# Splitting chained steps into single ones and writing out a new order of steps, in an SSD and feed-forward kernel

## The chip, the cores and the metric

The kernel runs on one core of one Trainium2 chip. A core has a matrix engine (TensorE, PE in the profile; its weight loads are listed as PEld), a vector engine (VectorE, DVE), a scalar engine (ScalarE, ACT), GpSimd (POOL) and a sync engine (SP), which in this kernel issues every transfer. Each engine works through its own instructions in the order in which the program gives them, and waits for the others by semaphores. The metric is the time of one execution on the device, in microseconds (us).

## The reference

First a state-space layer (Mamba-2, "SSD") over batch 4, 8 heads, 768 positions, head size 32, state size 16; then a gated feed-forward layer over the 3072 tokens that this gives, with 256 features and 1536 hidden ones:

```python
for c in range(nc):                                    # chunks of 32 positions
    cum = np.cumsum(la, axis=-1)                       # la = log of a
    L = np.exp(cum[:, :, :, None] - cum[:, :, None, :]) * causal
    M = np.einsum('bhin,bhjn->bhij', Cc, Bc) * L
    y_intra = np.einsum('bhij,bhjd->bhid', M, xc)
    y_inter = np.einsum('bhin,bhnd->bhid', Cc, state) * np.exp(cum)[:, :, :, None]
    y[:, :, sl] = y_intra + y_inter
    state = decay_full[:, :, None, None] * state + np.sum(Bx, axis=2)
...
rms = np.sqrt(np.mean(x * x, axis=-1, keepdims=True) + 1e-06)
xn = x / rms * rms_g
g = xn @ w_gate
silu = g * (1.0 / (1.0 + np.exp(-g)))
return silu * (xn @ w_val) @ w_out
```

The weights of the feed-forward layer arrive as 64-bit floating-point words; everything is computed in 32 bits.

## The kernel before, in words

**Blocks.** The 3072 tokens are six blocks of 512. Each block needs its part of the SSD (decays `L`, products `g` of B and C, states `A` and `S`, outputs `y`), then the norm (squares `sq`, their mean `ms` on PE, the root by ACT in `rs`, its spreading by transfers in `rb`, the normed tile `xn`), then the two input matrices (`gate` and `val`), the gating, and the output matrix.

**Weights.** The 64-bit words of 18 pieces are fetched and converted on the chip. Each piece k goes through `power(k)` (three dependent ACT steps, L217), `mantissa(k)` (two dependent DVE steps, L234 and L237) and `weight(k)` (one DVE step, L243, in steps called `wt`).

**Fast matrix products.** Most of the input products are done by a Strassen-like scheme: for each group j of 256 hidden features there are seven products `P.k.j` (L965) instead of eight. `P.1`, `P.4`, `P.6` and `P.7` add into one PSUM tile, `gate`, and `P.2`, `P.3` and `P.5` into another, `val`; there are two buffers of each. Between the products that add into `gate`, ACT copies the tile out (`take`, L971) and DVE adds such a copy to `val` (`C`, L977); then come the silu on ACT (L215) and the gating product (`hid`, L990, on DVE or POOL). A product is two 32-bit matmuls of 128x256, four in the profile. The sums of weights and of inputs that the scheme needs are L934 and L942. The output matrix has a scheme of its own: products `O` (L1086), sums of the hidden tiles (`u`, L1060) and totals (`w`, L1117 on DVE, L1113 on ACT), then `put`, the store. Part of block 0 is projected directly: `early` and `gate` steps (L879, L889), `norm` (L900), `hid` (L912) and `o` (L997).

**What sets the order.** No planner runs at build time. One string, `order`, lists the steps of the whole kernel, such as `0:P.1.5` (block slot 0, product 1 of group 5), and the loop at the end calls one function for each. Every engine, SP's transfers included, gets its instructions in that order. A number after a slash names the pair of PSUM banks for a step in the first part; after `switch` those banks hold the `gate` and `val` tiles. A step that issues several instructions puts them next to one another in their engine's queue. `rs.1` in slot 0, for example, is the square root of block 1's norm: Ln and Exp on ACT, and a transfer.

**The start.** `row sums` come first: `a` is loaded, turned (`aT`), limited (L351) and its logarithm taken; PE sums it (`r`), and `parts.0` (four dependent DVE steps, L411 to L417) splits the sums into three 16-bit parts; from these and a mask PE forms the exponents `e`, ACT the decays. In `order` the six loads of B and C (L143) stand near the beginning, then one pair of x, then `fetch.0` and `fetch.1`, which issue two transfers each (L185).

**ACT's tables.** `functions` (L202 to L209) remembers which set of functions is loaded, silu or exp and log, and puts in a load when a step needs the other one.

Of the kernel before, what the change touches and what calls it, by code (L numbers as in the profile page):

```python
# [10 lines left out]
I32 = mybir.dt.int32  # L11
# [9 lines left out]
def kernel(  # L21
# [195 lines left out]
    def power(k):  # L217
        words16, (lo, hi), dst, shape = fetched[k]
        n = shape[1] * shape[2]
        e = cvt.tile([P, n], FP32, tag="e", name="e", bufs=4)  # L220
# [3 lines left out]
        activation(out=k16, in_=words16, func=AF.Relu, scale=1.0 / 16, bias=kinks[:, 0:1])  # L224
        activation(out=g, in_=k16, func=AF.Prelu, scale=-1.0, bias=kinks[:, 1:2],
                             alpha=2.0 ** -20)
        activation(out=b16, in_=g, func=AF.Prelu, scale=-2.0 ** 27, bias=kinks[:, 2:3],
                             alpha=2.0 ** -20)
        parts[k, "e"] = b16.bitcast(BF16)

    def mantissa(k):
        words16, (lo, hi), dst, shape = fetched[k]
        m = cvt.tile(shape, I32, tag="m", name="m")
        nc.vector.tensor_scalar(out=m, in0=hi, scalar1=0xFFFFF, scalar2=0x100000,  # L234
                                op0=ALU.bitwise_and, op1=ALU.bitwise_or)
        parts[k, "f"] = f = m.bitcast(FP32)
        nc.vector.scalar_tensor_tensor(out=f, in0=lo.bitcast(U32), scalar=2.0 ** -32, in1=m,  # L237
                                       op0=ALU.mult, op1=ALU.add)
# [54 lines left out]
    def whole_chunks():  # L293
        nc.vector.memset(chunk_ones, 0.0)
        for u, r in enumerate(halves):
            nc.vector.memset(chunk_ones[r, u], 1.0)
# [12 lines left out]
    def of_quarters():  # L309
        nc.vector.tensor_scalar(out=three, in0=part[:, 3:4], scalar1=-1.0, scalar2=1.0,  # L310
                                op0=ALU.mult, op1=ALU.add)
        nc.vector.tensor_scalar_add(later_part, part[:, 0:1], -1.0)
        nc.vector.tensor_scalar(out=third_part, in0=part[:, 2:3], scalar1=-1.0, scalar2=None,
                                op0=ALU.mult)
# [4 lines left out]
    def from_middle():  # L319
        nc.vector.tensor_copy(out=mid, in_=upto)  # L320
        nc.vector.tensor_scalar_add(mid[0:HC], mid[0:HC], -1.0)

    def from_middles():
        nc.gpsimd.tensor_copy(out=mid, in_=upto)
        for r in halves:
# [3 lines left out]
        minus_mid()  # L329

    def mask16():
        for r in halves:
            nc.vector.tensor_copy(out=never16[r], in_=never[r, r])

    def kinks_of_powers():
        for k, v in enumerate((1152.0 - 7.5 / 16, 256.0, -1792.0 * 128.0)):
            nc.vector.memset(kinks[:, k:k + 1], v)
# [68 lines left out]
    def three_parts(k):  # L406
        r_ps = ps.pop(("r", k))
        room = nrm.tile([P, 4, P], FP32, tag="lead1", name="room", bufs=1)
        first, second = [room[:, k].bitcast(BF16).rearrange("p (s m) -> p s m", s=2)
                         for k in range(2)]  # L410
        nc.vector.tensor_copy(out=first, in_=r_ps)  # L411
        rest = room[:, 2:4]
        nc.vector.scalar_tensor_tensor(out=rest, in0=first, scalar=later_part, in1=r_ps,
                                       op0=ALU.mult, op1=ALU.add)
        nc.vector.tensor_copy(out=second, in_=rest)
        rows[k] = row = const.tile([P, 2, P], BF16, name="row%d" % k)
        nc.vector.scalar_tensor_tensor(out=row, in0=second, scalar=third_part, in1=rest,  # L417
                                       op0=ALU.mult, op1=ALU.add)
# [31 lines left out]
    def chunk_decays():  # L450
        activation(out=full.rearrange("p g h -> p (g h)"), in_=ps.pop("c"), func=AF.Exp)
        nc.gpsimd.tensor_tensor(out=fsel, in0=full,
# [52 lines left out]
    def causal(L):  # L505
        for r in halves:
            nc.gpsimd.affine_select(out=L[r], in_=L[r], pattern=[[0, L.shape[1]], [1, HC]],  # L507
                                    compare_op=ALU.is_ge, fill=0.0, base=0, channel_multiplier=-1)

    def spread(g):  # L510
        b, c = divmod(g, NC)
        o = (c * BH + b * NH) * HC
        for u, r in enumerate(halves):
            nc.sync.dma_start(out=pair_tile(g)[r].rearrange("p h m -> p (h m)"),
                              in_=rowv[u, o:o + NH * HC].partition_broadcast(HC))
# [8 lines left out]
    def exponential(g):  # L524
        L = pair_tile(g)
        activation(out=L, in_=L, func=AF.Exp)
        causal(L)

    def decays(g):
        subtract(g)  # L530
        exponential(g)
# [153 lines left out]
    def states(p):  # L685
        A_ps = ps.pop(("A", p))
        b, c0, chunks = chunks_of(p)
        new = ssd.tile([P, 2, 2, 2, D], FP32, tag="A", name="A")
        for u in range(2):
            n = sum(v == u for i, v in chunks)  # L690
            if n:
                nc.vector.tensor_tensor(
                    out=new[:, u, 0:n], in0=A_ps[u][:, 0:n],
# [799 lines left out]
```

## Time and profile before

| | |
|---|---|
| time, median of 3 runs (lowest, highest) | 391.32 us (391.13, 391.40) |
| span of the profiled execution | 389.5 us |
| PE busy | 383.3 us (98%) |
| DVE busy | 289.8 us (74%) |
| ACT busy | 226.4 us (58%) |
| POOL busy | 152.0 us (39%) |
| granted clock of PE | 1.00 throughout |

The span is one execution from its first to its last instruction as the profiler saw it; the time of a run is measured around the whole execution, 1.8 us more here. Times in rows count from the span's start. A row of the timeline gives start, length, engine, line, operation, output and inputs, and in brackets how long the engine had been idle and what it had been waiting for. Matmuls are pipelined: a group's length reaches beyond the start of the next one, and the distance from start to start is what the engine needs for one.

### The profile page before, as it was taken

To read this page: it belongs to the slowest core of one execution; us is meant where nothing else is said; L and a number is where in the kernel's file an instruction comes from. 1 tells how busy PE (TensorE), PEld (TensorE's weight loads), DVE (VectorE), ACT (ScalarE), POOL (GpSimd) and SP (SyncE) were. 2 spreads that over 40 slices of the span, in tenths; PEclk is the share of its full clock that TensorE was granted. 3 is DMA by queue.
4 is the path that set the end of the run, shared out by engine and by line. 5 is a ranking of instruction groups with operands and counts; after the bars stand their busy time and mean duration, and the time that the engine had idled before them with its cause. 6 is when DMAs were issued, how large, how long until landed. Compare 5 with 4: busy or idle time off the path is not lost.

```text
span 389.5 us, 9637 instructions
## 1 busy us (share of the span) xinstructions
PE 383.3 (98%) x3805; PEld 329.8 (85%) x3805; DVE 289.8 (74%) x612; ACT 226.4 (58%) x471; POOL 152.0 (39%) x168
## 2 busy tenths in 40 slices
PE   8999999999999999999999999999999999999996
PEld 5676478788888999888899988899888899988995
DVE  6999999997976988669594765768374577454684
ACT  2899979988767262665865234763444571345420
POOL 5022045523693455343577701364611234212231
PEclk9999999999999999999999999999999999999999
DMA  8978984474073414634336112000100001000001
GB/s 107 241 153 259 240 195 147 120 157 42 3 101 86 50 13 94 145 42 96 70 78 81 27 42 42 2 15 22 56 3 2 2 12 50 29 0 0 2 0 56
DMA packets 109940, 28.05 MB, mean 72 GB/s; under 512 B 94824, under 2 KB 103752, under 8 KB 109896
## 3 DMA queue, kind: packets, MB, share of 16 engines
q1 hardware_dynamic: 107816, 27.31, 32.8%
q8 instruction: 30, 0.49, 0.5%
q10 hardware_dynamic: 2080, 0.13, 0.4%
q14 instruction: 14, 0.11, 0.1%
HBM read 23.69 MB, written 3.74 MB: 70 GB/s over the span
## 4 chain that ended last, share of the span: by engine, by line
PE 87%; DVE 9%; issue 2%; ACT 1%; DVEq 0%; ACTq 0%
PE gate L965 29%; PE o L1086 23%; PE val L965 21%; PE o L997 5%; PE y L750 3%; PE g L613 1%; DVE wgv L243 1%; DVE m L237 1%; DVE m L234 1%; DVE hid L912 1%; PE g L606 1%; PE e L474 1%; PE y L678 1%; DVE L L652 1%; ACT yt L821 0%
## 5 line engine op out<-in xcount | busy, mean ns | idle before, releaser
L977 DVE TENSOR_TENSOR c<-val,p 128x512 f32<-128x512 f32 x99 | 67.4, 686 | 45.1 <-PE val L965 33.3
L971 ACT COPY p<-gate 128x512 f32<-128x512 f32 x99 | 56.8, 581 | 57.5 <-PE gate L965 55.4
L965 PE MATMUL gate<-tx,wgv 128*128 128x256 f32 x264 | 65.9, 381 | 0.0
L215 ACT ACTIVATE c<-c 128x256 f32<-128x256 f32 x99 | 40.0, 415 | 38.7 <-DVE c L977 38.4
L990 POOL TENSOR_TENSOR hid<-c 128x256 f32<-128x256 f32 x31 | 24.7, 800 | 87.1 <-ACT c L215 83.1
L965 PEld LDWEIGHTS gate<-tx,wgv 128*128 128x128 f32 x264 | 49.2, 190 | 7.3 <-ACT p L971 0.7
L1117 DVE TENSOR_TENSOR ob<-ob,o 128x128 f32<-128x128 f32 (+1 forms) x90 | 24.2, 298 | 21.7 <-PE o L1086 16.9
L990 DVE TENSOR_TENSOR hid<-c 128x256 f32<-128x256 f32 x68 | 34.5, 521 | 6.9 <-ACT c L215 6.7
L1086 PE MATMUL o<-two,hid 128*128 128x128 f32 x280 | 36.5, 276 | 0.1
L1086 PEld LDWEIGHTS o<-two,hid 128*128 128x128 f32 x280 | 34.5, 192 | 1.1 <-DVE hid L990 0.4
L965 PE MATMUL val<-xn,wgv 128*128 128x256 f32 x132 | 33.7, 381 | 0.0
L965 PE MATMUL val<-tx,sw 128*128 128x256 f32 x132 | 33.5, 380 | 0.0
L965 PE MATMUL val<-xn,sw 128*128 128x256 f32 x132 | 33.3, 381 | 0.0
L965 PE MATMUL gate<-tx,sw 128*128 128x256 f32 x132 | 33.1, 381 | 0.0
L965 PE MATMUL gate<-xn,wgv 128*128 128x256 f32 x132 | 32.8, 381 | 0.0
L507 POOL TENSOR_SCALAR_AFFINE_SELECT L<-L 64x512 f32<-64x512 f32 x32 | 23.6, 737 | 18.6 <-ACT L L215 17.4
L965 PEld LDWEIGHTS val<-xn,wgv 128*128 128x128 f32 x132 | 24.8, 190 | 3.5
L965 PEld LDWEIGHTS val<-tx,sw 128*128 128x128 f32 x132 | 24.8, 190 | 3.5 <-issue 0.2
L965 PEld LDWEIGHTS gate<-tx,sw 128*128 128x128 f32 x132 | 24.7, 190 | 3.5 <-ACT p L971 0.2
L965 PEld LDWEIGHTS gate<-xn,wgv 128*128 128x128 f32 x132 | 24.3, 190 | 3.4 <-DVE hid L912 0.3
L965 PEld LDWEIGHTS val<-xn,sw 128*128 128x128 f32 x132 | 24.4, 190 | 3.2 <-issue 0.2
L215 ACT ACTIVATE e<-e,kinks 128x512 f32<-128x512 int16 (+1 forms) x36 | 26.0, 722 | 1.2
(203 smaller groups left out, 717.0 us busy)
## 6 DMA issues: line engine op xcount, KB each, us to landing
L<-rowd SPq DMA_DIRECT2D x32, 128.0 KB, 3.4
xr<-in_x_dram SPq DMA_DIRECT2D x24, 128.0 KB, 3.2
wr<-in_moe_w_out_dram SPq DMA_DIRECT2D x6, 512.0 KB, 5.6
out_dram<-ob SPq DMA_DIRECT2D x24, 128.0 KB, 1.8
wr<-in_moe_w_gate_dram SPq DMA_DIRECT2D x5, 512.0 KB, 5.8
wr<-in_moe_w_val_dram SPq DMA_DIRECT2D x5, 512.0 KB
br<-in_B_dram SPq DMA_DIRECT2D x23, 64.0 KB, 2.6
dT<-rowe SPq DMA_DIRECT2D x10, 128.0 KB
```

The lines of the kernel that those rows point to most:

```text
L215: nc.scalar.activation(**operands)
L234: nc.vector.tensor_scalar(out=m, in0=hi, scalar1=0xFFFFF, scalar2=0x100000, op0=ALU.bitwise_and, op1=ALU.bitwise_or)
L237: nc.vector.scalar_tensor_tensor(out=f, in0=lo.bitcast(U32), scalar=2.0 ** -32, in1=m, op0=ALU.mult, op1=ALU.add)
L507: nc.gpsimd.affine_select(out=L[r], in_=L[r], pattern=[[0, L.shape[1]], [1, HC]], compare_op=ALU.is_ge, fill=0.0, base=0, channel_multipli ...
L750: nc.tensor.matmul(out=y[2 * k + u][rows, (2 * n + i) * HC:(2 * n + i + 1) * HC], start=(k, u, rows.start) not in opened, stop=True, skip_ ...
L965: nc.tensor.matmul(out=dst[:, half[w]], lhsT=lhsT, rhs=rhs, start=(k in (1, 2, 5) and w == 0), stop=True, skip_group_check=True)
L971: nc.scalar.copy(out=t, in_=Xs[j])
L977: nc.vector.tensor_tensor(out=t, in0=Zs[j], in1=a, op=ALU.add)
L990: engine.tensor_tensor(out=hid[:, 2 * j + c // 10 - 1, c % 10 - 1], in0=u, in1=src[:, half[1]], op=ALU.mult)
L997: nc.tensor.matmul(out=o, lhsT=hid[:, f, k // 2, (k % 2) * P:(k % 2 + 1) * P], rhs=wo[:, f], start=opens, stop=(f == NF - 1), skip_group_c ...
L1086: nc.tensor.matmul(out=Os[blk, b][:, place * P:(place + 1) * P], lhsT=hidden_or_sum(u)[:, g], rhs=rhs, start=(blk, b) not in opened, stop= ...
L1117: nc.vector.tensor_tensor(out=o, in0=o, in1=src, op=ALU.add if what[0] == "+" else ALU.subtract)
```

## The change

Functions that issue several instructions get an argument that picks one of them, and `order` names each separately. Split in this way are `power` (three), `mantissa` (two), `three_parts` (four), the constants of the start, the chunk decays (ACT step `cx`, POOL step `ch`), `exponential` (ACT step `ex`, and `ca`, the causal mask, for each half), `spread` (its two transfers), `states` (`Sn`, the new contributions, and `S`, one chunk each), `squares`, `taken_out` (`yt`), the norm's roots (`rs`), `norm_apply` (`xn`), `normed` and the last stores of block 0 (`putc`, `put`). The tile that a chain works on is now kept in a dictionary between its steps.

Then the whole string `order` is replaced. The instructions of PE, POOL and SP are the same ones in another order. DVE has one more (`xn` of block 0 in two halves), and ACT has 26 loads of a table instead of 22.

```diff
-    def mantissa(k):
+    def mantissa(k, stage):
         words16, (lo, hi), dst, shape = fetched[k]
-        m = cvt.tile(shape, I32, tag="m", name="m")
-        nc.vector.tensor_scalar(out=m, in0=hi, scalar1=0xFFFFF, scalar2=0x100000,
-                                op0=ALU.bitwise_and, op1=ALU.bitwise_or)
-        parts[k, "f"] = f = m.bitcast(FP32)
-        nc.vector.scalar_tensor_tensor(out=f, in0=lo.bitcast(U32), scalar=2.0 ** -32, in1=m,
-                                       op0=ALU.mult, op1=ALU.add)
+        if stage == 0:
+            parts[k, "m"] = m = cvt.tile(shape, I32, tag="m", name="m")
+            nc.vector.tensor_scalar(out=m, in0=hi, scalar1=0xFFFFF, scalar2=0x100000,
+                                    op0=ALU.bitwise_and, op1=ALU.bitwise_or)
+        else:
+            m = parts.pop((k, "m"))
+            parts[k, "f"] = f = m.bitcast(FP32)
+            nc.vector.scalar_tensor_tensor(out=f, in0=lo.bitcast(U32), scalar=2.0 ** -32, in1=m,
+                                           op0=ALU.mult, op1=ALU.add)
...
-    def states(p):
+    def states(p, n):
...
-    def norm_apply(blk):
+    def norm_apply(blk, t=0):
...
-            nc.vector.tensor_tensor(out=xns[0], in0=yts[0],
-                                    in1=r.unsqueeze(1).to_broadcast([P, 2, TB]), op=ALU.mult)
+            nc.vector.tensor_tensor(out=xns[0][:, t], in0=yts[0][:, t], in1=r, op=ALU.mult)
...
     order = """
-        0:warm 0:a 0:set 0:bc.0 0:ident 0:bc.1 0:bc2.1.1 0:ones 0:zeros 0:ident16 0:whole 0:kinks
-        0:idle.7 0:gcol 0:x.0 0:never 0:after 0:fetch.0 0:fetch.1 0:x.1 0:whole16 0:mask.0.0/0
-        0:part 0:hmask 0:upto 0:mid 0:mids 0:part2 0:aT 0:mask.1.1/2 0:la0 0:log4.0.4 0:upto2 0:r.0
-        0:fetch.2 0:head 0:sel 0:middles 0:after2 0:fetch.3 0:log4.4.2 0:log4.6.2 0:bc.3 0:tmask
-        0:parts.0 0:log 0:c*2 0:cx 0:mask.0.1/1 0:turn.0 0:Tb.0 0:T.0 0:d 0:dx 0:sums.0.1 0:sums.0.0
+        0:whole.0 0:warm 0:a 0:idle.7 0:ident 0:fetch.0 0:zeros 0:ones 0:ident16 0:kinks.1 0:upto
+        0:never 0:aT 0:whole16 0:fetch.1 0:mask.0.0/1 0:part 0:bc.0 0:whole.1 0:mid.0 0:upto2
+        0:mid.1 0:la0 0:kinks.0 0:never16.0 0:bc.1 0:never16.1 0:log4.0.4 0:mask.1.1/2 0:mids
+        0:whole.2 0:after 0:log 0:part2.2 0:bc2.1.1 0:r.0 0:part2.1 0:kinks.2 0:mask.0.1/0 0:part2.0
+        0:hmask 0:log4.6.2 0:after2 0:pow.0.0 0:head 0:man.0.0 0:log4.4.2 0:x.0 0:middles.0
+        0:parts.0.0 0:sel 0:parts.0.1 0:tmask 0:middles.1 0:d 0:parts.0.2 0:man.1.0 0:dx 0:middles.2
+        0:c*2 0:set 0:x.1 0:man.0.1 0:fetch.3 0:parts.0.3 0:pow.1.0 0:middles.3 0:r.1 0:cx 0:gcol
+        0:fetch.4 0:man.1.1 0:parts.1.0 0:fetch.5 0:scale.0.1 0:parts.1.1 0:sums.0.1 0:turn.0
...
-        0:silug.11.5 0:wt.12 0:hidgp.12.3 0:cw.0.1 0:ydone.2 0:silug.22.4 0:cw.1.2 0:fetch.17
-        0:spread.8 0:ms.1 0:take.6.5 0:P.7.5 0:rs.1 0:pow.13 0:sub.9 0:o.0/2 0:o.1 0:sub.10 0:man.13
-        0:fetch.14 0:hidg.21.4 0:take.7.5 0:wt.13 1:cwp.2.0 0:hidgp.22.3 0:cwp.0.3 0:C.22.5 0:P.4.5
+        0:sub.8 0:yt.3.2 0:man.14.0 0:ms.1 0:silug.21.4 0:take.6.5 0:rs.1.0 0:cwp.5.3 0:P.7.5
+        0:pow.15.1 0:rs.1.1 0:take.7.5 0:C.12.4 1:cwp.2.0 0:ex.10 0:o.0/2 0:P.4.5 0:pow.14.0
...
-        5:w.8 5:w.16 5:O.5.0 5:w.13 5:w.7 5:O.5.1 5:up.8 5:u.12 5:w.20 5:O.12.0 5:O.7.0 5:O.7.1
-        5:up.13 5:w.14 5:w.9 5:O.12.1 5:w.17 5:w.18 5:w.15 5:put.3 5:u.14 5:O.1.0 5:O.1.1 5:w.19
-        5:put.0 5:O.14.0 5:u.15 5:w.22 5:O.14.1 5:O.19.0 5:O.19.1 5:w.21 5:w.23 5:put.1 5:O.10.0
-        5:O.10.1 5:w.24 5:w.25 5:put.2
+        5:O.5.1 5:O.7.1 5:u.12 5:w.18 5:O.13.1 5:w.8 5:w.9 5:O.12.0 5:up.13 5:O.12.1 5:O.1.0 5:w.12
+        5:w.14 5:w.17 5:w.20 5:O.1.1 5:w.7 5:w.15 5:u.14 5:w.22 5:O.14.0 5:w.19 5:O.19.0 5:O.19.1
+        5:u.15 5:w.24 5:put.3 5:O.10.0 5:w.23 5:O.10.1 5:w.11 5:O.14.1 5:put.1 5:put.0 5:w.25 5:w.21
+        5:put.2
```

More of the change, by code (lines that the diff above doesn't have):

```diff
@@ L328, in from_middles, with mask16, kinks_of_powers @@
                                     scalar2=None, op0=ALU.add)
[L329 to L337, printed above, removed]
+    def mask16(k):
+        r = halves[k]
+        nc.vector.tensor_copy(out=never16[r], in_=never[r, r])
+    def kinks_of_powers(k):
+        nc.vector.memset(kinks[:, k:k + 1], (1152.0 - 7.5 / 16, 256.0, -1792.0 * 128.0)[k])
     def idle(n):
@@ L1144, in switch, with take @@
                          space=bass.MemoryType.PSUM))
[L1146 to L1151 removed]
+    def take(name):
+        return pair_of_banks(name, picks.pop(0))
     def start_decays(p, half=0):
[L1154 removed]
+        ps["e", p, half] = e = take("e")
         mask(p, e)
@@ L1223 @@
         "early": lambda f, s: products_early(
-            f, s, take("gate", ("gv", f)) if s == 0 else ps["gv", f]),
-        "norm": lambda f: (normed(f), leave(("gv", f))),
-        "gate": lambda f: products_gv(f, take("gate", ("gv", f))),
+            f, s, None if ("gv", f) in ps else take("gate")),
+        "norm": normed,
+        "gate": lambda f: products_gv(f, take("gate")),
         "silu": silu_of,
-        "hid": lambda f: (hidden(f), ("gv", f) in held and leave(("gv", f))),
+        "hid": hidden,
         "table": lambda k: functions("silu"), "switch": switch,
```

607 lines of the change are left out of this document (328 added, 279 removed).

## The prediction

> **What bounds the kernel now.** I read the span and the chain first, then busy time by stretch, then what DVE waits for, then DVE's, PE's and ACT's instructions one by one where the first big matrix products begin.
>
> From the page:
> ```profile
> span 389.5 us, 9637 instructions
> PE 87%; DVE 9%; issue 2%; ACT 1%; DVEq 0%; ACTq 0%
> ```
> The chain that ended last is PE for 87% of the span, and DVE's 9% is one stretch near the start. Busy time by stretch shows where (columns: stretch, length, then busy us and count for PE, PEld, DVE, ACT, POOL, then the clock, the DMA share, GB/s):
> ```profile
> 0.00:5.00 5.00, 3.86 (x13) 1.80 (x13) 3.14 (x21) 1.60 (x3) 2.41 (x12) 1.00 0.78 86
> 5.00:10.00 5.00, 4.91 (x38) 3.93 (x40) 3.47 (x11) 1.47 (x5) 2.60 (x5) 1.00 0.94 143
> 10.00:15.00 5.00, 5.00 (x64) 3.21 (x60) 4.57 (x11) 4.05 (x7) 0.00 (x0) 1.00 1.01 227
> 15.00:20.00 5.00, 4.35 (x112) 3.16 (x116) 4.78 (x11) 4.65 (x9) 0.00 (x0) 1.00 0.82 224
> 20.00:30.00 10.00, 9.93 (x150) 7.59 (x139) 9.59 (x23) 9.77 (x18) 2.18 (x2) 1.00 0.82 171
> 30.00:40.00 10.00, 9.96 (x61) 5.77 (x60) 9.86 (x18) 9.81 (x17) 2.25 (x3) 1.00 0.90 267
> 40.00:50.00 10.00, 10.00 (x141) 4.67 (x142) 9.69 (x22) 8.81 (x14) 0.00 (x0) 1.00 0.90 228
> 50.00:65.30 15.30, 14.80 (x286) 12.18 (x268) 14.69 (x32) 13.07 (x28) 9.04 (x11) 1.00 0.77 195
> ...
> 75.00:380.00 305.00, 304.85 (x2897) 274.40 (x2897) 216.22 (x436) 163.82 (x357) 129.38 (x131) 1.00 0.24 45
> ```
> DVE is full from 10 us until the products run, and idle before: 20 less 15.96 busy leaves 4.04 us of idle in the first 20, and 45.3 less 43.83 leaves 1.47 in the next 45.3. From 75 to 380 us PE is never without work (304.85 of 305.00). So only two things can move the time: when DVE gets its first 60 us of work done, and new stalls of PE later.
>
> What DVE waited for in 0 to 65.3 us (total, times, longest):
> ```profile
> DVE room L411 <- PE r_ps L402: 0.8, 1, 0.8
> DVE early L351 <- PE aT L347: 0.7, 1, 0.7
> DVE T L573 <- PE tp L554: 0.5, 1, 0.5
> ...
> DVE c L977 <- ACT p L971: 0.3, 1, 0.3
> DVE wgv L243 <- ACT e L215: 0.2, 1, 0.2
> ```
> The first three lie before 9 us. They and small gaps between dependent steps are the idle time.
>
> **Part one, the start.** The new order puts DVE steps that need nothing from the waited-for chain into those gaps: `mantissa` of pieces 0 and 1 (one L234 and one L237 each) and `parts.1` (four instructions, as `parts.0` has here). DVE's instructions, by start and length:
> ```profile
> 6.32 0.43 DVE L411 CAST room<-r_ps 128x256 bf16<-128x256 f32 x1 [0.83 <-PE r_ps L402]
> ...
> 7.70 0.48 DVE L417 SCALAR_TENSOR_TENSOR row<-room,third_part 128x256 bf16<-128x256 bf16 x1
> ...
> 60.86 0.69 DVE L237 SCALAR_TENSOR_TENSOR m<-wr,m 128x512 f32<-128x512 uint32 x1
> ...
> 62.07 0.69 DVE L243 SCALAR_TENSOR_TENSOR wgv<-m,e 128x512 f32<-128x512 f32 x1 [0.19 <-ACT e L215]
> 62.68 0.42 DVE L990 TENSOR_TENSOR hid<-c 128x256 f32<-128x256 f32 x1
> 63.02 0.69 DVE L977 TENSOR_TENSOR c<-val,p 128x512 f32<-128x512 f32 x1
> 63.62 0.68 DVE L912 TENSOR_TENSOR hid<-u,hid 128x512 f32<-128x512 f32 x1
> 64.22 0.41 DVE L990 TENSOR_TENSOR hid<-u,gate 128x256 f32<-128x256 f32 x1
> ...
> 65.55 1.24 DVE L702 SCALAR_TENSOR_TENSOR S<-S,fcol,A 128x64 f32<-128x64 f32 x4
> ...
> 68.47 0.42 DVE L234 TENSOR_SCALAR m<-wr 128x512 int32<-128x512 int32 x1
> 68.92 1.10 DVE L237 SCALAR_TENSOR_TENSOR m<-wr,m 128x512 f32<-128x512 uint32 x1
> ```
> Start to start, a 128x512 step takes 0.60 to 0.61 us of DVE (L243, L977, L912) and a 128x256 one 0.34, so `mantissa` twice is 2 x (0.42 + 0.61) = 2.1 us and `parts.1`, 6.32 to 8.18, at most 1.9: 4.0 us of filler against 4.04 of idle. It cannot all fit: the wait for the engine to start stays (0.89 us of `warm`), and the chain a, logarithm, row sums is as long as before. By hand 1.4 to 2.0 us of idle stay; I take **2.0 us won**, at most 2.6.
>
> The price is SP's queue. To have the weights by then, the four transfers of pieces 0 and 1 are issued ahead of six loads of B and C and the first of x:
> ```profile
> 7.51 0.58 SPq L185 DMA_DIRECT2D wr<-in_moe_w_gate_dram  x1
> ...
> 9.67 1.19 SPq L150 DMA_DIRECT2D xr<-in_x_dram  x2
> ```
> From 7.51 the four took 2.16 us to issue, so B and C start about that much later, behind 1 MB that the 227 GB/s of the 10 to 15 stretch moves in 4.6 us; DMA is already 0.78 to 1.01 busy. B and C of the first pair are needed after row 0 (8.18 us now, about 9.1 then, since `mantissa` stands ahead of `parts.0`), those of the second near 12.5. I find them about in time and charge nothing; if they are late by those 2.2 us, part one is worth nothing. That is the low end.
>
> **Part two, gaps between dependent steps.** Of the 1.47 us of idle from 20 to 65.3, the two named waits are 0.5; some 1.0 is gaps of 0.03 to 0.05 us (60.86 + 0.69 is already past the next start, 62.68 + 0.42 too, but a step that needs its predecessor's result starts only after it ends, as 68.92 after 68.47 + 0.42). With single steps another instruction stands between, and the last 0.08 us overlap. Between 0 and 1.0 I take **0.7 won**.
>
> **Part three, more work ahead of the tight point.** PE's instructions at the start of the products (start, length of the group, count):
> ```profile
> 65.29 1.03 PE L965 MATMUL gate<-xn,wgv 128*128 128x256 f32 x4
> 66.16 1.03 PE L965 MATMUL val<-xn,wgv 128*128 128x256 f32 x4
> ...
> 71.06 3.67 PE L997 MATMUL o<-wo,hid 128*128 128x256 f32 x16
> 74.75 1.13 PE L965 MATMUL gate<-tx,wgv 128*128 128x256 f32 x4
> ```
> The product at 65.29 (`P.1.5`) opens a gate tile that the `hid` sum at 64.22, done 64.63, must have left: 0.66 us of slack. In the new order DVE has, up to that same `hid`, two L234, one L237, one L243, one L520 and one L977 more, and one L702, one 128x256 L990 and one 128x256 weight sum less: 2 x 0.40 + 4 x 0.61 - 0.31 - 2 x 0.34 = 2.3 us more with the 0.06 that the split `xn` (two halves for one) adds. Beyond the slack that takes 2.3 - 0.66 = **1.6 us back**. So PE starts its unbroken run 2.0 + 0.7 - 1.6 = 1.1 us sooner. The L237 rows also show a price I leave at zero: the same step took 0.69 and 1.10, beside other work on POOL, and the new order may win or lose 0.4 at each such place.
>
> **Part four, ACT in the products.** A gate tile is copied by ACT (`take`, L971) before the next product may add to it. ACT's rows:
> ```profile
> 66.36 0.58 ACT L971 COPY p<-gate 128x512 f32<-128x512 f32 x1
> ...
> 70.06 1.28 ACT L209 ACT_TABLE_LOAD   x1
> 71.35 0.37 ACT L215 ACTIVATE r<-ms,eps 128x128 f32<-128x128 f32 x1
> 71.75 0.31 ACT L215 ACTIVATE r<-r 128x128 f32<-128x128 f32 x1
> 71.97 0.75 ACT L215 ACTIVATE e<-wr,kinks 128x512 int16<-128x512 int16 x1
> ...
> 74.13 0.56 ACT L971 COPY p<-gate 128x512 f32<-128x512 f32 x1
> ```
> The product of 65.29 is copied by 66.94; with one product between, PE, which starts a product every 0.87 us (65.29 to 66.16), would want the tile at 67.03. The old order has nearly always two products (1.73 us) or an `O` between; the new one has a single one at 19 places. With ACT free that costs nothing (0.09 less 0.06 to wake, as 74.69 to 74.75 shows); with an 0.37 ACT step in front it costs about 0.3. Bounds 0 to 19 x 0.3 = 5.7; I take 0.2, nearest to the free case, as ACT is busy 163.82 of 305 us, 54%, from 75 us on.
>
> Four table loads are added (22 to 26), 4 x 1.28 us on ACT. Three I find ahead of nothing that PE waits for, hidden by ACT's 46% of idle time; without that cover each would cost PE up to its 1.28. One, with Ln, a power step and Exp behind it, now stands directly ahead of the `take` that `P.4.5` waits for: 1.28 + 0.37 + 0.75 + 0.31 = 2.7 us. Before, PE already waited there (16 matmuls of 0.216 from 71.06 end at 74.52, the next came at 74.75). I take 0.2 more, bounds 0 to 0.6. The Trainium skill, page "ScalarE: Activation LUTs", section "What ACT_TABLE_LOAD costs", says that a switch costs 1283 ns and a drain of 1380 ns besides. The trace does not agree with the second: the load at 70.06 ended at 71.34 and Ln started at 71.35. By the page the stall would be 1.4 us larger.
>
> **Part five, the tail and the rest.** The end of block 5 is reordered as well:
> ```profile
> 382.51 1.16 PE L1086 MATMUL o<-sw,hid 128*128 128x128 f32 x8 [0.38 <-DVE ob L1117]
> ```
> As I read the order, the total L1117 that this product waits for now stands ahead of one more product, so the wait goes: 0.3 won, bounds 0 to 0.4. The last product, total and store are others than before but of the same kinds and lengths. Engines' work is otherwise the same instruction for instruction; finer steps of POOL and SP are hidden by PE after 65 us. If not, each late transfer would cost its issue, 0.5 us.
>
> **The sum.** -1.1 (start) + 0.2 (takes) + 0.2 (table) - 0.3 (tail) = -1.0 us. The profiled execution's span of 389.5 becomes 388.5. The median of the runs is 391.3, 1.8 more than the span, which I carry over: **390.4 us** (-0.2%). A measurement of this kernel can tell 0.2%, or 0.8 us, from no change: faster is under 390.5, slower over 392.1.
>
> **Rivals.**
> 1. The whole start pays: 2.6 + 1.0 - 1.6 = 2.0 less, and 0.3 at the tail, no stalls: 389.0. For it: the filler equals the idle time. Against: the chain of row sums has its own length.
> 2. No change: B and C land late by half of those 2.2 us, part one gives 1.0 instead of 2.0, and the sum is 0.0: 391.4. Late by all of it, the start costs 1.6 - 0.7 = 0.9, and the sum is +1.0, 392.3. For it: DMA share 0.94 to 1.01. Against: row 0, which comes first, is itself 0.9 later.
> 3. Slower, one mechanism: ACT arrives late at the 19 places with one product of cover. The sum without them is -1.2, so it turns the sign from 0.06 us a place and passes 0.2% from 0.1; at 0.2 it is 3.8 - 1.2 = +2.6, **393.9**, at the full 0.3 396. For it: a margin of 0.03 us. Against: ACT's mean load.
>
> By the page's drain the table load alone gives -1.0 + 1.4 = +0.4, 391.7, a case like rival 2; with the Ln row against it I give it 0.02 of that rival's chance.
>
> **How the numbers follow.** Forecast (389.4 to 390.9 by the bounds of its terms) 0.40, rival 1 0.16, rival 2 0.18, rival 3 0.26. The range, 388.2 to 393.6, reaches past rival 1's 389.0 by what the gaps of DVE could still give, and up to nearly the middle case of rival 3; above it lies about half of that rival, 0.14, below it 0.05. Faster: 0.16 and 0.33 of the 0.40, together 0.49; the same: the other 0.07 and 0.15 of rival 2, 0.22; slower: 0.26 and 0.03, 0.29.
>
> **What would show it.** In the new profile DVE should be busy some 18 of the first 20 us; the four weight transfers should precede B and C; the first unbroken products should stand about 1 us earlier; ACT should show 26 table loads. Waits of PE (or its weight loads) for ACT L971 totalling over 2 us, or DVE idle for transfers between 8 and 13 us, would make the forecast wrong.

## The result and the profile after

The changed kernel takes 421.07 us (median of 5 runs, 419.59 to 422.88) against 391.13 us (5 runs, 391.03 to 391.40): ratio 1.0775, 95% interval 1.0752 to 1.0798. The forecast was 390.4 us, with a range up to 393.6: the kernel is 30 us slower where a gain of 1 was expected. The profiled execution is the slowest of the five, 422.88 us with a span of 421.0; the other four have spans of 417.7 to 419.9.

From the page of the changed kernel (span, PE and its neighbours, granted clock in tenths over 40 slices, chain):

```profile
span 421.0 us, 9645 instructions
PE 393.8 (94%) x3805; PEld 330.9 (79%) x3805; DVE 297.7 (71%) x613; ACT 230.4 (55%) x475; POOL 154.6 (37%) x168
PEclk9998999998999999999999999989999999999999
PE 65%; DVE 12%; SPq 8%; DMA 7%; issue 3%; POOL 2%; ACT 2%; DVEq 0%; POOLq 0%; ACTq 0%
```

PE now stands in the chain for 65% instead of 87%, and two things are there that were not: SP's queue (SPq) with 8% and transfers (DMA) with 7%. PE is idle for 27.2 us instead of 6.2 (421.0 - 393.8, 389.5 - 383.3), and busy 10.5 us longer for the same 3805 matmuls. About 5 of the 10.5 are its clock, whose mean is 0.988 (421 x 0.012); what the rest is stays open. What PE waited for (total, times, longest):

```profile
PE val L1002 <- DVE xn L897: 5.2, 2, 3.9
PE o L1123 <- DVE ob L1154: 4.1, 4, 1.3
PE o L1123 <- DVE hid L1097: 2.9, 2, 2.5
PE y L700 <- DMA xr<-in_x_dram: 2.0, 2, 1.5
PE g L635 <- DVE T L609: 1.7, 1, 1.7
PE y L777 <- DVE L L674: 1.5, 1, 1.5
PE idle L359 <- DVE warm L385: 1.4, 1, 1.4
```

Before, four waits were listed, 2.5 us together. Now there are many, of many kinds, from one end of the kernel to the other. Busy time by stretch, the first and the long one as in the prediction (columns as there):

```profile
0.00:5.00 5.00, 3.55 (x13) 1.96 (x14) 2.79 (x22) 1.99 (x4) 2.34 (x12) 1.00 0.66 152
5.00:10.00 5.00, 4.43 (x34) 3.13 (x33) 4.15 (x13) 3.32 (x6) 2.47 (x5) 1.00 0.92 161
10.00:15.00 5.00, 4.27 (x54) 2.87 (x53) 4.91 (x11) 3.78 (x6) 0.92 (x1) 1.00 0.94 124
15.00:20.00 5.00, 5.00 (x83) 3.38 (x86) 4.42 (x11) 4.37 (x9) 0.00 (x0) 1.00 0.90 287
75.00:420.00 345.00, 327.84 (x2989) 287.47 (x2987) 235.72 (x468) 175.35 (x374) 133.48 (x133) 0.99 0.21 42
```

PE was never without work from 75 us on; now it is for 17.2 us (345 less 327.84).

**Where the time goes.** To place the loss I took PE's instructions of each kernel in their order, gave each the start-to-start time that its kind has in the trace of before, and called the sum the work. The lag is how much later than in the trace of before PE reaches the same amount of work, in us. Whether a kind is weighed by its mean or its median moves the entries by up to about 1 us, so smaller differences say nothing. The kernels beside the changed one are experiments of the next section.

| work done | changed | e3 | e4 | e5 |
|---|---|---|---|---|
| 30 | 0.2 | 0.0 | 0.1 | 0.2 |
| 60 | 8.7 | 4.0 | 4.5 | 3.4 |
| 80 | 14.9 | 11.6 | 4.5 | 5.3 |
| 100 | 14.9 | 11.6 | 12.5 | 5.6 |
| 140 | 17.1 | 11.6 | 14.7 | 7.9 |
| 180 | 22.1 | 13.0 | 19.4 | 14.1 |
| 220 | 24.0 | 13.0 | 21.4 | 16.1 |
| 260 | 30.6 | 13.0 | 26.6 | 22.7 |
| 360 | 31.3 | 12.9 | 27.3 | 23.4 |

The first 30 us of work take what they took, within that 1 us. The changed kernel's 8.7 at 60 has about 4 us of a wait at 39 us (the `T` L609 row above, and a low clock behind it) that the traces of e3, e5, e6, e7 and e10, which have the same order there, do not show: it comes and goes with one transfer, issued at 32.45 and landed at 38.64 here. Half of the loss is there by 80 us of work, the other half comes in single steps until 260. The largest step of the first half is at 86 to 98 us:

```profile
80.93 0.30 ACT L215 ACTIVATE r<-r 128x128 f32<-128x128 f32 x1
...
81.33 4.18 SPq L541 DMA_DIRECT2D L<-rowd  x6
85.61 0.54 SPq L883 DMA_DIRECT2D roots<-r  x1
...
86.88 0.69 DVE L547 TENSOR_TENSOR L<-L,tok 128x512 f32<-128x512 f32 x1 [3.34 <-DMA L<-rowd]
...
87.04 1.89 PE L1034 MATMUL o<-wo,hid 128*128 128x256 f32 x8
...
88.49 1.75 SPq L888 DMA_DIRECT2D sq<-roots  x4
...
91.99 1.41 DVE L897 SCALAR_TENSOR_TENSOR xn<-yt,gcol,sq 128x512 f32<-128x512 f32 x2 [1.83 <-DMA sq<-roots]
...
92.80 1.13 PE L1002 MATMUL val<-xn,wgv 128*128 128x256 f32 x4 [3.87 <-DVE xn L897]
94.06 3.67 PE L1034 MATMUL o<-wo,hid 128*128 128x256 f32 x8
```

The root of block 1's norm is done by ACT at 81.23. Its transfer to DRAM (`rs.1.2`, L883) is issued at 85.61, 4.4 us later, because SP is still issuing six spreads of decays (L541), 0.7 us each, that stand ahead of it. DVE, in its own order, stands at 86.88 behind a spread that landed late, then waits for the roots themselves; PE waits 3.87 us. The eight matmuls at 94.06 then take 3.67 us where the eight at 87.04 took 1.89: PE's clock has dropped to half. In the profile before, the same two transfers were:

```profile
72.09 0.35 SPq L847 DMA_DIRECT2D roots<-r  x1
...
74.20 1.95 SPq L852 DMA_DIRECT2D sq<-roots  x4
```

Counted in SP's rows (ACT's queue issues two more transfers, the first loads of B and C, so it is not quite all that SP issues), 64 transfers stood ahead of `roots` before, and 90 stand ahead of it now: 7 spreads, 12 squares, 4 of B, 2 of x and one weight more. Before, SP had nothing else to do and waited 8.8 us for the root; now the root waits 4.4 us for SP. The other 9.2 of the 13.5 us by which `roots` goes out later are the root's own lateness (done at 81.23 instead of 72.06), most of which the lag of 8.7 at 60 us of work already holds. In e3, which lacks the wait at 39 us, the root is done at 76.44 and issued at 81.63, 5.2 us later. The 13.5 us can't be divided into a price for each transfer: 72 of the 90 rows take 0.55 us on average, 18 are longer than 1 us, up to 4.26, and why these are longer is not shown. The DMA engines' share from 33 us to there (to 73 and to 86) rose from 0.70 to 0.83, with the same 183 and 184 GB/s.

### The profile page after: what moved, and what is told of

It is laid out like the page before. It is cut to its first block, busy times and chain, and to the rows that moved or that the text cites. A ratio compares the mean times of both kernels' runs of the same rounds, so it can differ in the third digit from the quotient of the medians.

```text
span 421.0 us, 9645 instructions
## 1 busy us (share of the span) xinstructions
PE 393.8 (94%) x3805; PEld 330.9 (79%) x3805; DVE 297.7 (71%) x613; ACT 230.4 (55%) x475; POOL 154.6 (37%) x168
## 4 chain that ended last, share of the span: by engine, by line
PE 65%; DVE 12%; SPq 8%; DMA 7%; issue 3%; POOL 2%; ACT 2%; DVEq 0%; POOLq 0%; ACTq 0%
PE gate L1002 22%; PE val L1002 15%; PE o L1123 14%; PE o L1034 4%; SPq L133 3%; PE gate L914 2%; DVE xn L897 2%; PE gate L926 2%; DMA dT<-rowe 1%; SPq L541 1%; DVE hid L1027 1%; PE g L635 1%; PE y L777 1%; DVE hid L1097 1%; DMA sq<-roots 1%
## 5 line engine op out<-in xcount | busy, mean ns | idle before, releaser
L1002 PE MATMUL gate<-tx,wgv 128*128 128x256 f32 x264 | 66.8, 384 | 0.0
L215 ACT ACTIVATE c<-c 128x256 f32<-128x256 f32 x99 | 38.8, 415 | 22.9 <-DVE c L1014 22.5
L1123 PE MATMUL o<-two,hid 128*128 128x128 f32 x280 | 39.4, 277 | 0.3 <-DVE hid L1097 0.3
L1123 PEld LDWEIGHTS o<-two,hid 128*128 128x128 f32 x280 | 35.7, 192 | 1.8 <-issue 0.6
L1002 PE MATMUL gate<-xn,wgv 128*128 128x256 f32 x132 | 34.3, 386 | 2.0 <-DVE hid L949 0.9
L1027 DVE TENSOR_TENSOR hid<-c 128x256 f32<-128x256 f32 x68 | 32.6, 492 | 4.7 <-ACT c L215 4.6
L1002 PE MATMUL val<-xn,sw 128*128 128x256 f32 x132 | 34.5, 388 | 1.0 <-DVE c L1014 1.0
```

Of the source, the lines that this page charges most:

```text
L215: nc.scalar.activation(**operands)
L1002: nc.tensor.matmul(out=dst[:, half[w]], lhsT=lhsT, rhs=rhs, start=(k in (1, 2, 5) and w == 0), stop=True, skip_group_check=True)
L1027: engine.tensor_tensor(out=hid[:, 2 * j + c // 10 - 1, c % 10 - 1], in0=u, in1=src[:, half[1]], op=ALU.mult)
L1123: nc.tensor.matmul(out=Os[blk, b][:, place * P:(place + 1) * P], lhsT=hidden_or_sum(u)[:, g], rhs=rhs, start=(blk, b) not in opened, stop= ...
```

## The experiments

**e1: splitting alone.** The order of before, with every split chain written as its single steps next to one another.

```diff
-        0:take.6.5 0:P.7.5 0:rs.1 0:pow.13 0:sub.9 ... 0:man.13
+        0:take.6.5 0:P.7.5 0:rs.1.0 0:rs.1.1 0:rs.1.2 0:pow.13.0 0:pow.13.1 0:pow.13.2 0:sub.9 ... 0:man.13.0 0:man.13.1
```

> The changed kernel's single steps, put in the order of the kernel before (each old step's single steps side by side; block 0's normed tile still in two halves). Theory A (the new order alone makes the loss, the splitting costs nothing): 391.1 within 0.5 us, 22 table loads. Theory B (the splitting itself costs, by the extra instruction and the way tiles are held between steps): a good part of the 30 us, over 400 us.

Measured: 391.28 us, ratio 1.0014 (0.9999 to 1.0028). DVE's extra instruction is there (x613), the stretches are those of before. That is theory A: at most 1 us of the 30 (the upper end of the interval) comes from the finer functions, the rest is the new order.

**e2 and e3: one half old, one half new.** The order was cut at the first products of the block after block 0 (about 92 us). e2 has the old order up to there and then what is left in the new order, e3 the reverse. In outline:

```diff
-    order = new
+    order = old up to 1:P.*.0, then the steps of new that are not yet done      (e2)
+    order = new up to 1:P.*.0, then the steps of old that are not yet done      (e3)
```

> The old order up to the first product of the next block (about 82 us), then all that is left in the new order. The new order falls behind by 14.9 us up to there, by PE's instructions against the same work in the kernel before. Theory A (the losses are local, each at its place): 421 - 15 = 406 us. Theory B (a queue that overflows at the start, SP's, drags on and causes the later losses too): near 391 to 396 us.

> The reverse: the new order up to the first product of the next block (about 92 us), then what is left in the old order. Theory A (local losses): 391 + 15 = 406 us. Theory B (the start's overflow causes the rest): near 415 to 421 us.

e2 took 423.36 us (1.0838, 1.0801 to 1.0876), slower than either theory said. Its trace has no lag up to 80 us of work, and then one stall, with its cause on DVE:

```profile
PE gate L1002 <- DVE tx L979: 15.1, 1, 15.1
...
95.28 0.69 DVE L547 TENSOR_TENSOR L<-L,tok 128x512 f32<-128x512 f32 x1 [11.05 <-DMA L<-rowd]
```

The rest of the new order assumes that SP has issued the later blocks' transfers already. With the old start it has not, so they are all due at the junction and SP issues them without a gap from 78.17 to 99 us. The stall is made by the cut; what e2 shows is the same cause at another place: the transfers are work that SP must do at some time, and where they stand ahead of one that is needed, PE stops. Behind it e2 loses another 14 us in steps, as the changed kernel does.

e3 took 404.64 us (1.0358, 1.0325 to 1.0390), as theory A said (406). Its lag is 11.6 at 80 us of work, with the same chain (DVE waits 3.86 for a spread, 2.03 for the roots, PE 5.67 behind both, here named by the weights that DVE makes after `xn`), and grows by 1.3 in the remaining 280:

```profile
82.57 0.69 DVE L547 TENSOR_TENSOR L<-L,tok 128x512 f32<-128x512 f32 x1 [3.86 <-DMA L<-rowd]
...
89.82 5.53 PE L1034 MATMUL o<-wo,hid 128*128 128x256 f32 x16 [5.67 <-DVE wo L252]
```

So the 16.4 us that the changed kernel loses from 80 to 360 us of work are due to the new order of that part, not to what the start leaves behind; the 14 us that e2 loses there with the old start agree.

**e4: the transfers moved behind the roots.** 15 steps, which issue 24 transfers for later blocks, now follow `rs.1.2` and `rb.1`; seven steps that read what they bring are moved back with them.

```diff
-        0:Sn.2.0 0:sq2.2.0.2 0:wt.6 ... 0:S.2.2 0:pow.8.2 0:fetch.13 0:x.4 0:man.8.0 0:sq2.2.0.1 ...
+        0:Sn.2.0 0:wt.6 ... 0:S.2.2 0:pow.8.2 0:fetch.13 0:x.4 0:man.8.0 ...
+        (behind 0:rs.1.2 and 0:rb.1)  0:sq2.2.0.2 0:sq2.2.0.1 ...
```

> The new order, with 24 transfers for later blocks (squares, loads of B, of x, spreading of row sums) issued behind the norm's transfers of block 1 (roots, then its spreading) instead of ahead of them, and the six steps that read them moved back as well; roots is then transfer 67 of SP instead of 91 (65 in the kernel before). Theory A (SP's queue, which issues one transfer every 0.55 us, makes the root late): roots is issued by 78 us instead of 85.6, the wait of PE for the normed tile (3.9 us) and the lower clock behind it (about 2 us) go, together with some waits for B and row sums before it: 6 to 9 us less, 412 to 415. Theory B (the root is late because Ln and Exp are, on ACT behind a table load and a power step): within 1.5 us of 421.

Measured: 420.16 us (1.0742, 1.0686 to 1.0798).

```profile
77.02 0.35 SPq L883 DMA_DIRECT2D roots<-r  x1
...
99.18 0.45 DVE L580 STREAM_TRANSPOSE T<-squares 128x256 f32<-128x256 f32 x1 [7.60 <-DMA squares<-in_B_dram]
```

The first half of theory A holds: the root goes out as soon as it is done (76.99), 8.6 us sooner than in the changed kernel (4.2 of them because it is done sooner, as the wait at 39 us is mostly absent from this trace), and the lag stays at 4.5 through 80. The second does not: the moved squares are late in turn, DVE stands 7.60 us before one, PE 5.7 behind it, and by 100 the lag is 12.5. Moving the transfers past one another only chose who waits: the queue has too many of them in this stretch. The median is 0.9 us below the changed kernel's, with overlapping intervals.

**e5: a second queue.** The squares of block 2 and the spreads of groups 12 to 15 are issued by POOL, the order is unchanged.

```diff
-                nc.sync.dma_start(
+                (nc.gpsimd if blk == 2 else nc.sync).dma_start(
...
-        nc.sync.dma_start(out=pair_tile(g)[r]...
+        (nc.gpsimd if 12 <= g < 16 else nc.sync).dma_start(out=pair_tile(g)[r]...
```

> The new order unchanged, but 24 of the transfers of the first 95 us (16 of the squares, 8 of the spreading of row sums) are issued by GpSimd's queue instead of SP's. Theory A (SP can only issue one transfer per 0.55 us, and the new order asks for 26 more of them before the root of block 1): with 18 fewer in front, roots is issued by 78 us instead of 85.6, and the transfers don't come due later as in the run where they were only moved back; 8 to 13 us less, 408 to 413. Theory B (the DMA engines themselves are full, whoever issues): within 2 us of 421.

Measured: 414.62 us (1.0615, 1.0572 to 1.0657), below the interval of the changed kernel, though above the range that theory A gave.

```profile
76.27 0.35 SPq L883 DMA_DIRECT2D roots<-r  x1
```

The root, done at 76.24, goes out at once; in e3, which has the same order up to there and like e5 lacks the wait at 39 us, it is done at 76.44 and waits 5.2 us. The lag at 80 us of work is 5.3, against 11.6 in e3, and it stays (5.6 at 100): the late `xn` and the low clock behind it are gone. The DMA engines had no less to do: from 33 to 76 us their share is 0.94 here and 0.87 in e3, at 204 and 193 GB/s. So the first half's largest step was SP's queue and not the transfers' bandwidth. The bytes are the same, but the packets are not: POOL's 24 transfers run in a DMA queue of another kind (software_dynamic on its page, hardware_dynamic for SP's) and as 896 packets, where the same 24 were 9088 in SP's. The time of all packets hardly changes by it (31.0% of the changed kernel's 421.0 us, 29.6% and 1.8% of 413.2 us in e5). The Trainium skill, page "DMA: Bandwidth & Descriptors", section "Issuing engines are not separate DMA queues", says that transfers run on the same 16 DMA engines whoever issues them, and that a second issuer saves only the time of issuing, which is usually small beside the transfer. Here it was not small: 5.2 us for one finished root. The later part is unchanged: 18.1 us more from 80 to 360 (16.4 in the changed kernel).

**e9: all of them on POOL.** The same for every block and group.

```diff
-                nc.sync.dma_start(
+                nc.gpsimd.dma_start(
...
-        nc.sync.dma_start(out=pair_tile(g)[r]...
+        nc.gpsimd.dma_start(out=pair_tile(g)[r]...
```

> The new order, with the transfers of squares and the spreading of row sums of all blocks issued by GpSimd's queue, not only those of the first stretch. Theory A (SP's queue also makes the later losses): PE's waits for x near 200 us (2 us) and for the normed tile near 226 us (1.5 us), and the stall at 155 us (2 us) whose chain begins with late squares, go as well: 4 to 7 us less than with the first stretch alone (414.6), 408 to 411. Theory B (the later losses come from the order of products and sums): 413 to 416.

Measured: 429.52 us (1.0993, 1.0969 to 1.1016): slower, against both theories.

```profile
PE 395.2 (92%) x3805; PEld 331.9 (78%) x3805; DVE 304.8 (71%) x613; ACT 230.4 (54%) x475; POOL 214.8 (50%) x280
...
PE o L1123 <- POOL s L1097: 2.7, 1, 2.7
```

POOL's rows here count the issuing: 112 of them add 60 us, and POOL works in order too. Its sums (L1097) now stand behind transfers, and its transfers behind steps that wait (the longest 17.7 us). In this kernel POOL could take 24 transfers and not 112. Whether SP's queue also makes part of the later losses is left open by this run.

**e6: POOL's sums on DVE.** To see whether instructions of POOL slow DVE, all 38 hidden sums that the changed order gives to POOL (`up`) were given to DVE (`u`).

```diff
-        1:up.3 ... 1:up.4 ... 1:up.5
+        1:u.3 ... 1:u.4 ... 1:u.5
```

> The new order with all 38 sums of hidden tiles that GpSimd computes (L1097, 0.7 to 1.3 us each there) put on VectorE in the same place. Theory A (in the later blocks DVE is slowed by GpSimd's sums that run beside it: hid at 276.9 us took 1.65 for two instead of 0.8, the sum at 278.9 took 1.78 instead of 0.68, and PE waited 2.5 us for it): DVE's instructions return to their short times, the waits of PE for DVE hid L1097 and ob L1154 shrink, 3 to 8 us less, 413 to 418. Theory B (DVE's queue is simply too full there): 38 x 0.6 = 23 us more on DVE, at least 2 us slower, over 423.

Measured: 420.26 us (1.0742, 1.0719 to 1.0765): neither theory. At 280 us, the largest step of the second half, the changed kernel has:

```profile
278.91 1.26 POOL L1097 TENSOR_TENSOR s<-hid 128x512 f32<-128x512 f32 x1 [1.03 <-DVE hid L1027]
...
278.93 1.78 DVE L1097 TENSOR_TENSOR hid<-hid 128x512 f32<-128x512 f32 x1
...
280.77 0.71 PE L1123 MATMUL o<-wo,hid 128*128 128x128 f32 x4 [2.51 <-DVE hid L1097]
```

The sum on DVE started 0.02 us after one on POOL and took 1.78 us, against 0.68 for a sum of that size alone (L912 in the prediction's rows). By groups from 100 to 380 us (busy us, mean ns), the state steps in the profiles of before, of the changed kernel and of e6:

```profile
L702 DVE SCALAR_TENSOR_TENSOR S<-S,fcol,A 128x64 f32<-128x64 f32 x20 | 6.2, 308 | 0.6
```

```profile
L729 DVE SCALAR_TENSOR_TENSOR S<-S,fcol,A 128x64 f32<-128x64 f32 x26 | 14.3, 551 | 0.2
```

```profile
L729 DVE SCALAR_TENSOR_TENSOR S<-S,fcol,A 128x64 f32<-128x64 f32 x25 | 7.9, 316 | 0.2
```

With POOL's sums gone the mean falls back from 551 to 316 ns, so the slowing is POOL's. Summed over the whole kernel, DVE's instructions take 34.7 us more than the lower quartile of their form (21.5 before, 22.9 in e6). The Trainium skill, page "SBUF — State Buffer", section "Who interferes with whom", says that a DVE instruction with two SBUF inputs contends with a GpSimd instruction that reads SBUF, and calls the use of the ports that they share an exclusive lock. The rows agree (1.78 is POOL's 1.26 and 0.52 more, somewhat less than one such step). But those 11.8 us did not come back as time: at 280 the lag grew by 1.8 instead of 4.6, and DVE, with 38 sums more, was late elsewhere. As e6 adds work to DVE while it ends the slowing, what the slowing alone costs is not shown.

PE's waits for these sums and for the totals in e6:

```profile
PE o L1123 <- DVE s L1097: 4.2, 3, 2.1
...
PE o L1123 <- DVE ob L1154: 2.4, 5, 0.9
```

**e7 and e10: one late step moved.** Two waits of the second half that looked like a single misplaced step.

```diff
-        2:spread.1.1 2:silu.11.2 2:x.0 2:hid.11.2 ... 2:hid.22.1 2:x.1 2:silu.22.3        (e7)
+        2:spread.1.1 2:silu.11.2 2:x.0 2:x.1 2:hid.11.2 ... 2:hid.22.1 2:silu.22.3
...
-        3:O.4.0 3:hid.12.4 ... 3:O.3.1 3:O.4.1                                           (e10)
+        3:hid.12.4 ... 3:O.3.1 3:O.4.0 3:O.4.1
```

> The new order with one step moved: the load of x for the second pair of block 3, from 7 steps before its use to 43 steps before it, ahead of 13 transfers. Theory A (PE's wait of 2.0 us for x near 200 us is SP's queue again): the wait goes, 1.5 to 2.5 us less. Theory B (it is hidden or replaced by the next wait, for the state sums behind it): less than 0.7 us.

> The new order with one product moved: the first half of O.4 of block 3, for which PE waits 2.5 us at 278 to 281 us, stands directly ahead of its second half (17 steps later), as in the kernel before. Theory A (the product stands too close behind the sum that it reads, and products that are ready wait behind it; the wait also costs 1.6 us of lower clock): wait and low clock go, 3 to 4 us less, 417 to 418. Theory B (DVE is late by then in all it does): the next product waits instead, less than 1 us.

Measured: 418.61 us (1.0707, 1.0682 to 1.0731) and 419.41 us (1.0740, 1.0712 to 1.0767). In both the wait that was aimed at went, and another took its place; the last row of each shows it (e7, then e10):

```profile
PE val L1002 <- DVE c L1014: 2.8, 2, 1.8
```

```profile
278.22 1.13 PE L1002 MATMUL val<-xn,sw 128*128 128x256 f32 x4 [2.66 <-DVE c L1014]
```

By the traces that is theory B twice: the instructions behind the moved step are late as well. For e10 the median, 1.7 us below the changed kernel's, fits neither theory, and the lag at the place grows as it did. For e7 it is not settled: its trace is of the slowest of five runs (421.74), the other four took 417.92 to 419.01, and the median, 2.5 us lower, is what theory A gave. None of these gains is shown to be the moved step's own, since the wait at 39 us, which neither trace has, comes and goes between traces.

**e12: e5 with one silu moved ahead of ACT's single power steps.**

```diff
-        0:pow.11.0 0:pow.10.0 0:S.2.0 0:pow.8.0 0:S.2.1 0:pow.8.1 0:man.10.0 0:silu.5 0:wt.9
+        0:pow.11.0 0:pow.10.0 0:S.2.0 0:silu.5 0:pow.8.0 0:S.2.1 0:pow.8.1 0:man.10.0 0:wt.9
```

> As e5_pool_queue (the squares of block 2 and the spreads of groups 12 to 15 issued from POOL), with one step moved: ACT's silu.5 of block 0 stands ahead of the five single steps of `power` that stood before it. In e5 DVE waited 1.6 us for that silu and PE 1.15 us behind it at 51.5 us. Theory A (splitting `power` let the order put ACT's small steps ahead of a silu that the takes need, and that is a loss of its own): both waits go, and the time is 1 to 2 us below e5's 414.6, so 412.6 to 413.6. Theory B (the next late thing, `wgv` of the spreads, takes the place of the wait 2.5 us later): within 0.7 us of 414.6.

Measured: 413.39 us (1.0576, 1.0540 to 1.0612). The median is where theory A put it, 1.2 below e5's, but the intervals overlap and the trace shows no gain at the place. PE's waits from 40 to 75 us, of e5 and then of e12:

```profile
PE gate L1002 <- DVE hid L949: 1.2, 1, 1.2
PE val L1002 <- DVE c L1014: 1.0, 1, 1.0
PE gate L1002 <- DVE wgv L252: 0.7, 1, 0.7
```

```profile
PE val L1002 <- DVE c L1014: 0.8, 1, 0.8
PE gate L1002 <- DVE wgv L252: 0.7, 1, 0.7
...
PE gate L1002 <- DVE hid L949: 0.5, 1, 0.5
```

The wait fell from 1.2 to 0.5, and the lag at 60 us of work is 3.7 against e5's 3.4: nothing was won there. The 1.0 us between their spans arises at 190 us, where e5's trace shows a low clock and e12's does not. Whether the split of `power` cost anything is left open at the size of 1 us.

**e8: the predicted gain at the tail, alone, in the kernel before.**

```diff
-        5:up.8 5:u.12 5:w.20 ... 5:O.12.1 5:w.17 5:w.18 5:w.15
+        5:up.8 5:u.12 5:w.18 5:w.20 ... 5:O.12.1 5:w.17 5:w.15
```

> The kernel before with one step of block 5 moved: the total 18 (DVE, L1117), which PE waits for at 382.5 us, from behind totals 14, 9 and 17 to the place ahead of total 20. Theory A (the 0.55 us wait at the end is only the order of DVE's totals): 0.3 to 0.5 us less than before, ratio 0.999. Theory B (the next total is then late instead): no difference.

Measured: 391.01 against 390.72 us (1.0003, 0.9989 to 1.0016). In the trace the product that stood at 382.51 with a wait of 0.38 starts at 381.95 without one; the interval is too wide to tell 0.3 us from nothing.

**e11: the price of one wait.** The kernel before, with 30 small writes of an unused tile on DVE ahead of one total of block 3.

```diff
+        "pad": lambda blk, n: [nc.vector.memset(warm, 0.0) for _ in range(n)],
-        3:O.7.0 3:w.18
+        3:O.7.0 3:pad.30 3:w.18
```

> The kernel before with 30 small fills (0.17 us each, of a tile that nothing reads any more) put on DVE ahead of one total of block 3 that PE needs, so that PE waits once for some microseconds near 265 us; nothing else is changed. Theory A (a wait of PE of more than about 2 us costs half the clock for some 3 us behind it): if PE waits for w us, the time grows by w + 1.5 to 2, and the windows behind the wait show a clock of about 0.7 over 5 us. Theory B (the low clock in the changed kernel has another cause): it grows by w and the clock stays at 1.00.

Measured: 400.54 us (1.0249, 1.0227 to 1.0272), 10.1 above before. PE waits once, and the stretch behind it (clock in the third column from the end):

```profile
PE gate L965 <- ACT ob L215: 6.9, 1, 6.9
...
275.00:280.00 5.00, 3.22 (x11) 2.86 (x12) 2.46 (x11) 2.90 (x6) 2.74 (x4) 0.50 0.02 5
```

The span grew by 8.9 us to 398.4, the median by 10.1: a wait of 6.9 us costs its length and 2 to 3 more, while the clock is 0.50. So theory A has the kind right, with a lower clock than its 0.7. The order behind it gives nothing back: the lag stays at 9 to the end.

No kernel tried here is faster than the one before.

## Why the prediction was wrong, point by point

- **The start (parts one to three, -1.1).** The order worked as said: the four weight transfers precede B and C, and B and C were not late. No row of the first 30 us waits for them. But no gain shows: at 45 us of work the lag is -0.1 to -0.2 in e5 and e6, which lack the wait at 39 us, and that is less than two traces of one order differ (`ms` of block 1 starts at 69.70 in the trace of before and at 69.31 in e1's). The products, which were to stand 1 us earlier, lag by 3.4 or more at 60 us of work in every column of the table. DVE is busy 16.27 of the first 20 us, not 18: its first filler waited 0.75 us for its own weights, and the wait for `warm` grew from 1.1 to 1.4. The terms were too large by about 1.0. (Their sum would give 390.3, 391.3 less 1.0, and not 390.4; nothing hangs on it.)

```profile
6.25 0.43 DVE L241 TENSOR_SCALAR m<-wr 128x512 int32<-128x512 int32 x1 [0.75 <-DMA wr<-in_moe_w_val_dram]
```

- **ACT in the products (part four, rival 3).** From 66 us on, weight loads waited for takes 17 times, 3.7 us in total and 0.3 at the longest, where before it was 3 times and 0.9:

```profile
PEld gate L1002 <- ACT p L1008: 3.7, 17, 0.3
```

  That is the sign which the prediction named for rival 3, and it cost at most 2.8 of the 30 us; the matmuls themselves list no wait for it above 0.2. The 26 table loads are there, and PE lists no wait behind them. ACT was not what failed.
- **The tail (part five, -0.3).** The mechanism is right in e8's trace; the time can't tell so small a gain from none. In the changed kernel another total is waited for near the end, 0.7 us at 408.87.
- **The step that failed** is in part five: "Engines' work is otherwise the same instruction for instruction; finer steps of POOL and SP are hidden by PE after 65 us. If not, each late transfer would cost its issue, 0.5 us." The price per transfer was near (0.55 for four rows of five, the rest longer), but the number was never taken: SP's queue was followed up to 13 us and not to the roots of block 1, where 26 more transfers stand ahead of one that PE needs within some 10 us, so that a finished root waits 4.4 us (5.2 in e3) to be issued. e5 shows that this place alone is worth some 6 us (11.6 in e3 against 5.3 at 80 us of work; medians 421.07 against 414.62). "Hidden by PE" also took the one unbroken run of PE as a property of the work, while it was one of the order: e1 keeps the order and the run, e3 restores both after 92 us and loses 1.3 instead of 16. For "new stalls of PE later" the sum had 0.4 us, takes and table, all of them on ACT; from 75 us on PE now stands idle for 17.2 us, and the longest of these waits are for DVE and for transfers.
- **A term set at zero:** POOL beside DVE. Part three saw an L237 step at 0.69 and at 1.10 and left it at nothing. It grew by 13.2 us of DVE's time (34.7 less 21.5). e6 wins it back and the median falls by only 0.8 us, but with 38 more sums on DVE; so what this term is worth by itself stays open.
- **A term not thought of:** the clock. Every wait of PE was priced at its length. About 5 of the 30 us are what the half clock behind three of them cost.

**What stays open.** That the second half's 16 us come from the order of the later blocks is shown by e3. How they divide among late squares, sums of POOL, the late load of x and misplaced products is not: e6, e7 and e10 each removed one wait and got another. Open too are the 3.4 us by which e5 lags at 60 us of work: PE's four waits for DVE from 40 to 75 us add up to them (1.2, 1.0 and 0.7 in the rows above, and 0.5 for `L`), but only one of their causes was tried, in e12, without a gain at its place.

## What to carry to other kernels

When an order is written anew, count for each in-order queue what stands ahead of the transfer or step that the bounding engine needs next, SP's queue first: here 26 more transfers of half a microsecond and longer ahead of one decided more than all the fillers of DVE. An unbroken run of the bounding engine is the slackless result of one order; a reordering puts at risk all of that run, so the comparison has to go through it to the end, and not only through the stretch that the change is meant for. Removing one wait of such a kernel tells little while the next instruction is as late.

## What the runs showed of the hardware that was not expected

**Half clock behind short waits.** The wait of 2.51 us at 280.77 is followed by a stretch with a granted clock of 0.68 in the changed kernel, and its next four matmuls take 1.87 us instead of 1.03:

```profile
280.00:285.00 5.00, 4.23 (x24) 3.02 (x25) 4.48 (x9) 2.10 (x7) 3.57 (x4) 0.68 0.02 3
```

The waits of 1.54 us at 200.28 and 1.32 at 226.83 left it at 1.00, but in e5 waits of 1.22 and 0.44 us for x left 0.66 in the stretch from 190 to 195. The length alone does not decide. In the changed kernel the clock is 0.50 in three stretches (39.46 to 42.87, 94.07 to 97.49, 281.81 to 285.22), each 3.41 us long, and their starts lie 16 and 55 times 3.413 us apart. On that grid, PE is idle for 1.71, 2.27 and 2.37 us of the 3.41 just before them, and for 1.66 of those before e5's drop at 191.61; the wait before 226.83 fills only 1.32 of its 3.41, and the one before 200.28 is cut at 199.89 into 1.14 and less. So the idle part of such a stretch seems to decide, without a sharp limit: 1.73 us in the stretch that ends at 90.66 left the clock at 1.00. The Trainium skill, page "TensorE: Matmul & The Clock Gate", section "Part 1: The HAM clock gate", says that the clock halves after at least one idle window of about 3.4 us, that the window runs freely, and that some 3.4 us of work bring the full clock back. The half rate (0.50), the 3.41 us of it and the fixed grid agree; that PE need be idle for only about half of such a window does not.

**Issuing costs the issuer.** Most of SP's 251 rows in the changed kernel take 0.34 to 0.63 us of its queue (median 0.49), with no order by size: 32 KB of squares mostly 0.49, 512 KB of the output matrix 0.40 to 0.53 in five of six. But 25 are over 1 us, up to 4.26. POOL spends 0.52 to 0.88 us of its working time on a transfer (60 us for 112 in e9).
